# Two cost constants of a planner, and the order of TensorE's 965 units, in an attention and feed-forward kernel on one core

## The chip, the core and the metric

The kernel runs on one core of a Trainium2 chip. The metric is device time in microseconds (us) of one execution. The profile is that of one execution, with every instruction and every DMA packet of the core.

## What is computed

Eight batches of twelve heads, sequence 448, head dimension 64. Scores are mixed across heads before the softmax and again after it, and the result goes through a feed-forward layer with a squared ReLU:

```python
scores = scale * q @ k.T                              # (8, 12, 448, 448)
scores = einsum('bhij,hg->bgij', scores, w_pre)       # mix heads
attn   = softmax(scores)
attn   = einsum('bhij,hg->bgij', attn, w_post)        # mix heads again
x      = (attn @ v), heads side by side               # (3584, 768)
out    = relu(x @ w_in) ** 2 @ w_out                  # 768 -> 2048 -> 768
```

## The kernel before

**Work and its stages.** TensorE's work is cut into 965 units, each a few matmuls into one or two PSUM banks, plus warm-up matmuls that the planner puts into early gaps. The kinds of units, by the start of their names, with the lines that show them in the profile:

- `tr` (L832, L836): transposes of q and k of a batch.
- `spr` (L915): scores of the first 320 query rows of batch 0, made directly in the mixing layout.
- `qk` (L974, L981, L988): scores of a tile of 128 query rows, two heads at a time, six units a tile. A batch has four tiles; the fourth has 64 rows, is made by three units, and has line L974 to itself. Each score block is copied from PSUM into `stage` by ScalarE or VectorE (`fn_sev`).
- Relayout (`emit_rel`, `rel` tasks): DMAs issued by SyncE (SP) move ten query rows of all twelve heads from `stage` to a slot of `dring`, so that heads lie on partitions. Rows of a 128-row tile take one DMA (L1035); rows of the 64-row tile take two (L1033), here called split relayouts. A batch has eight of these.
- `pre` (L1059, L1066, L1074): the first head mixing, from `dring`. ScalarE makes the exponentials with their row sums (L1099), GpSimd (POOL) the reciprocal (L1122) and the scaled second mixing matrix (L1132).
- `post` (L1164): the second head mixing, which also transposes; its result goes to `a2t`.
- `av` (L1221, L1242): attention times v, to `xt`. `h` units (L1293, L1301): the first feed-forward matmul; its ReLU (L1338, L1339) and square (L1348) go to `h2t`. `o` units (L1440; L1380 and L1432 at the end): the second feed-forward matmul, a half of the contraction each. Its result goes to `osb` and is stored by SP (L1478).

Buffers that tie these together: `stage` has two slots, so a tile's copies wait until the relayouts of the tile before the last one have landed; `dring` has 16 slots; `osb` has two, so an output tile's copy waits until the store of the tile two before has landed.

**What sets the order.** No order is written by hand. At build time `_Plan` plays the program through with a cost for each task and gives every engine a list; semaphores are placed by those lists, and the chip runs each list in order. TensorE's sequence is a string, `ORDER`: each character names the stream (`s_T`, `s_QK`, `s_pre`, ...) from which the next unit is taken, and which of up to three array shapes it takes: whole array (`full`), halves by rows (`row`), or quarters (`quad`); `av` units have a shape of their own (`cols`), `spr` units too (`c32`). The string was found by a search that minimises the planned span. All other engines' lists follow from it in `run`: the next task is the one that can start first, and a copy goes to ScalarE or VectorE as the planner expects it to end sooner.

**The planner's costs that matter here.** A change of array shape between units costs `MODE_SWITCH`, 100 ns. TensorE's instructions come in blocks of 256; `fetch` says how long after entering a block the next one is there, with parts for loads and relayouts that are under way. Every relayout holds SP for 1000 ns, whether of one DMA or split:

```python
t = plan.add("rel%d_%d_%d" % (b, c, d0), SP, fn, sev_of[n],
             {SP: (1000.0, 0.0)}, g * 1.0, sem, 32 if two else 16,
             dma=("move", 10.0 + 73.3 * nv, 54.0))
```

The end of a relayout is the end of its modelled transfer plus `DMA_END["move"]` (`dma_next`).

Of the kernel before, what the change touches and what calls it, by code (L numbers as in the profile page):

```python
# [19 lines left out]
MODE_SWITCH = 100.0  # L20
ACT_BIAS = 14.5
BLOCK = 256
FETCH = (2700.0, 2300.0, 1500.0)
EVENTS = {"tr": 0.12, "qk": 0.72, "di": 0.2, "sp": 0.3, "po": 0.61, "pr": 1.1, "av": 0.43, "o0": 0.43}
DMA_START = {"move": 2590.0, "load": 2640.0, "big": 1680.0}
DMA_AHEAD = 1600.0
DMA_END = {"move": 1450.0, "load": 1300.0}
INF = float("inf")
CODES = "0123456789abcdefghijklmnopqrst"
ORDER = (  # L30
    "00005bb05b0555555555555555555c12c555555513223555552c5001c353c00153355255233355555b332c22"
    "44443002h1g1b2q1h332g2236gh313c6722133hh31233gh6131hb2424443b32g26gh7q2b7371c63q1711r736"
    "2qh32002932t121j33933282b2s3c83338004224441200bgh11181c3s311s133s322rghg22b72b6h3163q633"
    "q32r42244413rbbh2ggb2002h716371623763q223837c738c33i3832bgh112rg0204244b20041328111ic31i"
    "3c3i33911tc11t22bj3c393c39342414431j313j2bqb2b62731762236733h3200q2162r21h13633g32r22728"
    "02000s131i113i14242b4334222931t333t111922813i3138422443411i332q2b6b2r2brb2gq0023733r3633"
    "qbrbq2rg2r200bh22913j12009111j3c381c383c3s313sc342442224193139111t333t2422444228318131i3"
    "13s32q2bqr227b3h2b2g733q333q20b6r120h2q0262000h7119331t111j33ct2228383138131ib4242224418"
    "3138331i24244413832q2bq2r2bh236331q33hgb21g72000r102h2173633633h24244420ttb2092b9238111i"
    "133i333i2t22btb2btbb2t238338331i42244431s31q2262713r1161733qh32qb2g2r2b273733r33gg12s22i"  # L40
    "22ss42244483i33s33i2qr262h2933933t33jq4q444hgqg6rgqhrh7ihgh6hgrhgg7hrqjjsjjit8isitijj"
)


# [72 lines left out]
class _Plan:  # L117
# [86 lines left out]
    def dma_next(self, go=False):  # L204
# [26 lines left out]
        if go:  # L231
# [5 lines left out]
            self.moving[t.dma[0]].pop(0)  # L237
            t.end = max(t.end, now + DMA_END[t.dma[0]])
            self._finish(t)
# [10 lines left out]
    def fetch(self, at):  # L250
        part = {}
        for q, xs in self.moving.items():
            part[q] = min(1.0, sum(x[1] for x in xs if x[0] <= at + 500.0) / 2500.0)
        return FETCH[0] + FETCH[1] * part["load"] + FETCH[2] * part["move"]

# [1442 lines left out]
```

## Time and profile before

| | |
|---|---|
| Runs, median (lowest to highest of 3) | 539.58 us (534.83 to 539.79) |
| The profiled execution: its time, its span | 537.8 us, 536.0 us |
| Mean granted TensorE clock | 0.988 |
| Busy in the span: PE, ACT, DVE, POOL | 508.0, 412.3, 379.9, 290.8 us |
| Matmuls | 10441 |
| Instruction packets on the queue that serves TensorE | 86, of 16 KB |

The span runs from the first to the last instruction; the profiled execution's time is 1.8 us more. PE is TensorE's matmuls, SP the engine that only issues DMAs. "Idle before" names what ended a wait; "issue" means that the engine waited for nothing that the profile shows.

### The profile page before, as it was taken

To read this page: it belongs to the slowest core of one execution; us is meant where nothing else is said; L and a number is where in the kernel's file an instruction comes from. 1 tells how busy PE (TensorE), PEld (TensorE's weight loads), DVE (VectorE), ACT (ScalarE), POOL (GpSimd) and SP (SyncE) were. 2 spreads that over 40 slices of the span, in tenths; PEclk is the share of its full clock that TensorE was granted. 3 is DMA by queue.
4 is the path that set the end of the run, shared out by engine and by line. 5 is a ranking of instruction groups with operands and counts; after the bars stand their busy time and mean duration, and the time that the engine had idled before them with its cause. 6 is when DMAs were issued, how large, how long until landed. Compare 5 with 4: busy or idle time off the path is not lost.

```text
span 536.0 us, 24801 instructions
## 1 busy us (share of the span) xinstructions
PE 508.0 (95%) x10441; PEld 332.8 (62%) x10441; DVE 379.9 (71%) x806; ACT 412.3 (77%) x1181; POOL 290.8 (54%) x524
## 2 busy tenths in 40 slices
PE   8979999999999889989999899999989999989996
PEld 4435676667776546656566565666547766657963
DVE  7868977797987678765878768876857868536510
ACT  5979998888977878887787798888857888955421
POOL 9837788427954667446843587336844345522000
PEclk9989999999999999999999999999989999998999
DMA  9998999547964689457973689447963467532013
GB/s 172 192 184 145 196 183 193 112 87 146 178 154 75 137 183 173 93 127 135 180 166 67 140 150 224 92 91 163 193 134 64 105 141 142 113 72 61 3 29 93
DMA packets 81997, 70.87 MB, mean 132 GB/s; under 512 B 14038, under 2 KB 78422, under 8 KB 81878
## 3 DMA queue, kind: packets, MB, share of 16 engines
q1 hardware_dynamic: 48326, 46.40, 35.8%
q0 software_dynamic: 33392, 22.59, 31.0%
q8 instruction: 86, 1.41, 1.1%
q14 instruction: 33, 0.27, 0.1%
q10 hardware_dynamic: 160, 0.20, 0.1%
HBM read 45.63 MB, written 11.01 MB: 106 GB/s over the span
## 4 chain that ended last, share of the span: by engine, by line
PE 76%; DMA 7%; ACT 5%; DVE 4%; SPq 3%; issue 3%; POOL 0%; DVEq 0%; POOLq 0%
PE ps L1440 20%; PE ps L1301 17%; PE ps L1293 9%; PE ps L1164 6%; PE ps L1074 6%; DMA dring<-stage 5%; PE ps L1242 5%; SPq L1033 3%; ACT pring L1099 3%; PE ps L988 3%; PE ps L1380 2%; PE ps L1432 2%; PE ps L915 2%; DVE stage L524 2%; PE ps L836 2%
## 5 line engine op out<-in xcount | busy, mean ns | idle before, releaser
L1122 POOL TENSOR_TENSOR rinv<-rowsum,minus 128x2 f32<-128x2 f32 (+1 forms) x179 | 125.2, 702 | 185.9 <-ACT pring L1099 185.1
L1099 ACT ACTIVATE pring<-ps 128x448 bf16<-128x448 f32 x360 | 192.6, 563 | 23.0 <-PE ps L1074 13.2
L524 DVE CAST a2t<-ps 128x480 bf16<-128x480 f32 (+1 forms) x209 | 126.6, 641 | 37.6 <-PE ps L1164 36.7
L1440 PE MATMUL ps<-w_out_sb,h2t 64*128 64x384 bf16 (+1 forms) x1728 | 141.7, 324 | 0.2
L524 DVE CAST stage<-ps 128x448 bf16<-128x448 f32 x168 | 99.9, 618 | 31.1 <-PE ps L981 11.4
L1301 PE MATMUL ps<-xt,w_in_sb 64*64 64x448 bf16 (+4 forms) x1728 | 109.5, 329 | 0.1
L1440 PEld LDWEIGHTS ps<-w_out_sb,h2t 64*128 64x128 bf16 (+1 forms) x1728 | 75.3, 97 | 43.3 <-issue 2.0
L523 ACT ACTIVATE a2t<-ps 128x480 bf16<-128x480 f32 (+1 forms) x159 | 85.9, 580 | 20.8 <-PE ps L1164 20.0
L523 ACT ACTIVATE stage<-ps 128x448 bf16<-128x448 f32 x138 | 72.2, 556 | 18.7 <-PE ps L988 6.5
L1099 ACT ACTIVATION_READ_ACCUMULATOR pring<-ps 128x1 f32 x360 | 81.8, 227 | 0.0
L1301 PEld LDWEIGHTS ps<-xt,w_in_sb 64*64 64x64 bf16 (+1 forms) x1728 | 60.4, 103 | 29.8 <-issue 2.3
L1164 PEld LDWEIGHTS ps<-wk2s,pring 60*128 60x128 bf16 x2880 | 57.4, 94 | 28.0 <-issue 7.1
L1132 POOL TENSOR_TENSOR wk2s<-wk2b,rinv 128x120 bf16<-128x120 bf16 (+1 forms) x179 | 69.0, 388 | 10.2
L1164 PE MATMUL ps<-wk2s,pring 60*128 60x60 bf16 x2880 | 64.8, 187 | 4.4 <-issue 2.6
L1348 DVE TENSOR_TENSOR h2t<-h1t 128x448 bf16<-128x448 bf16 (+2 forms) x176 | 54.7, 336 | 11.2 <-ACT h1t L1338 10.1
L1074 PE MATMUL ps<-dring,wk 64*64 64x448 bf16 (+1 forms) x592 | 53.0, 360 | 10.0 <-DMA dring<-stage 3.4
L1293 PE MATMUL ps<-xt,w_in_sb 128*128 128x220 bf16 (+2 forms) x480 | 59.1, 276 | 0.0
L1338 ACT ACTIVATE h1t<-ps 128x448 bf16<-128x448 f32 (+2 forms) x88 | 39.1, 450 | 20.4 <-PE ps L1293 11.2
L1339 DVE TENSOR_SCALAR h1t<-ps 128x448 bf16<-128x448 f32 (+2 forms) x88 | 42.7, 492 | 16.5 <-PE ps L1301 13.1
L1293 PEld LDWEIGHTS ps<-xt,w_in_sb 128*128 128x128 bf16 x480 | 43.8, 98 | 12.3 <-issue 2.8
L523 ACT ACTIVATE osb<-ps 128x384 f32<-128x384 f32 x31 | 15.1, 492 | 27.2 <-PE ps L1432 8.6
L1242 PE MATMUL ps<-a2t,vraw 128*64 128x228 bf16 (+1 forms) x640 | 35.2, 261 | 0.0
(78 smaller groups left out, 464.5 us busy)
## 6 DMA issues: line engine op xcount, KB each, us to landing
dring<-stage SPq DMA_DIRECT2D x264, 105.0 KB
out_dram<-osb SPq DMA_DIRECT2D x45, 192.0 KB, 3.5
qraw<-in_q_dram POOLq DMA_DIRECT2D x42, 112.0 KB, 5.1
kraw<-in_k_dram POOLq DMA_DIRECT2D x42, 112.0 KB, 5.1
dring<-stage SPq DMA_DIRECT2D x70, 52.5 KB
w_in_sb<-in_moe_w_in_dram POOLq DMA_DIRECT2D x8, 384.0 KB, 10.0
w_out_sb<-in_moe_w_out_dram POOLq DMA_DIRECT2D x8, 384.0 KB, 8.8
vraw<-in_v_dram POOLq DMA_DIRECT2D x21, 128.0 KB
```

Of the source, the lines that this page charges most:

```text
L523: return eng.activation(o, i_, AF.Copy)
L524: return eng.tensor_copy(o, i_)
L1074: r_ = eng.matmul(ps[64 * y:64 * y + 64, gr.banks[x], 0:S], wk1[64 * x:64 * x + 64 - R0 * x, 64:128], dring[64 * x:64 * x + 64 - R0 * x, ( ...
L1099: return eng.activation(pring[:, pr, 0:S], ps[:, gr.banks[x], 0:S], AF.Exp, accum_out=rowsum[:, g, :])
L1122: return eng.tensor_tensor(rinv[:, p0:p0 + n, :], rowsum[:, g0:g0 + n, :], minus1[:, 0:n, :], ALU.pow)
L1132: return eng.tensor_tensor(wk2s[:, p0:p0 + n, :], i0.to_broadcast([128, n, PR]), rinv[:, p0:p0 + n, :].to_broadcast([128, n, PR]), ALU.mult)
L1164: r_ = eng.matmul(ps[:, gr.banks[x], o0:o0 + PR], pring[64 * x:64 * x + PR, pr + y, j0:j0 + 2 * PJ], wk2s[64 * x:64 * x + PR, pr + y, :], ...
L1242: r_ = eng.matmul(ps[kk * 64:kk * 64 + 64, g.banks[x_], x * n:(x + 1) * n], vraw[:, h, s, :], a2t[half][:, s, h, a0:a0 + n], start=(rest a ...
L1293: r_ = eng.matmul(ps[:, g.banks[ph], 0:n], w_in_sb[:, ft, t * 128:(t + 1) * 128], xt[:, ft, c0:c1], start=(ft == 0), stop=(ft == NFT - 1))
L1301: r_ = eng.matmul(ps[z:z + w, g.banks[x], 0:n], w_in_sb[64 * y:64 * y + 64, ft, t * 128 + z:t * 128 + z + w], xt[64 * y:64 * y + 64, ft, c ...
L1348: return eng.tensor_tensor(h2t[:, t16, o0:o0 + n], h1t[:, s, 0:n], h1t[:, s, 0:n], ALU.mult)
L1440: r_ = eng.matmul(ps[z:z + w, g.banks[hh], 0:FH], h2t[64 * y:64 * y + 64, t16, col + z:col + z + w], w_out_sb[64 * y:64 * y + 64, t16, hh ...
```

## The change

Two planner constants are raised: the base of an instruction fetch from 2700 to 3500 ns, and the time from a relayout's modelled end to its arrival from 1450 to 2000 ns. `ORDER` is replaced by another string of the same units. No other line differs, so all work is the same; what changes is its sequence on every engine, the array shapes of some units, and which of ScalarE and VectorE makes some copies.

```diff
-FETCH = (2700.0, 2300.0, 1500.0)
+FETCH = (3500.0, 2300.0, 1500.0)
...
-DMA_END = {"move": 1450.0, "load": 1300.0}
+DMA_END = {"move": 2000.0, "load": 1300.0}
...
 ORDER = (
-    "00005bb05b0555555555555555555c12c555555513223555552c5001c353c00153355255233355555b332c22"
+    "000b051010155555515555555555555c2552c5530055533c255553b22c50505553335c532c5535533155c4b4"
...
```

Two places show how the sequence moves.

The first is on PE where batch 2 ends and batch 3 begins. L974 with `qkt` is the 64-row score tile of batch 2; L988 and L981 are the score tiles of batch 3, six units each; L1440 is a half of an output tile, L1293 a piece of the first feed-forward matmul, L1074 the first head mixing. Before, from the last unit of the 64-row tile on:

```order
L974 MATMUL ps<-qkt 64x448 x8
L1074 MATMUL ps<-dring,wk 64x448 x4
L1293 MATMUL ps<-xt,w_in_sb 128x228 x12
L836 MATMUL ps<-ident,qraw 64x64 x28
L1074 MATMUL ps<-dring,wk 64x448 x4
L836 MATMUL ps<-ident,kraw 64x64 x28
L1221 MATMUL ps<-a2t,vraw 64x220 x8
L1074 MATMUL ps<-dring,wk 64x448 x4
L1242 MATMUL ps<-a2t,vraw 64x220 x24
L981 MATMUL ps<-qkt 64x448 x4
```

Now, from the same unit on:

```order
L974 MATMUL ps<-qkt 64x448 x4
L836 MATMUL ps<-ident,kraw 64x64 x28
L1221 MATMUL ps<-a2t,vraw 64x220 x8
L1074 MATMUL ps<-dring,wk 64x448 x4
L1242 MATMUL ps<-a2t,vraw 64x220 x24
L836 MATMUL ps<-ident,qraw 64x64 x28
L836 MATMUL ps<-ident,kraw 64x64 x28
L1074 MATMUL ps<-dring,wk 64x448 x4
L988 MATMUL ps<-qkt 128x448 x2
L1440 MATMUL ps<-w_out_sb,h2t 128x384 x16
L988 MATMUL ps<-qkt 128x448 x2
```

The feed-forward piece, a transpose and two head mixings now stand ahead of the 64-row tile; with them gone from behind it, the tiles of batch 3 follow it sooner.

The second is on SP at the same place. L1033 are the eight split relayouts of batch 2 (16 DMAs), L1035 the relayouts of whole tiles, L1478 the stores of output tiles (32 rows each for batch 0, 64 for batch 1). Before:

```order
L1035 DMA dring<-stage 48x1x448
L1478 DMA out_dram<-osb 32x768 x3
L1033 DMA dring<-stage 36x1x448 x2
L1033 DMA dring<-stage 60x1x448 x10
L1033 DMA dring<-stage 24x1x448 x4
L1478 DMA out_dram<-osb 32x768
L1478 DMA out_dram<-osb 64x768 x2
L1035 DMA dring<-stage 120x1x448 x12
```

Now:

```order
L1035 DMA dring<-stage 48x1x448
L1478 DMA out_dram<-osb 32x768 x4
L1478 DMA out_dram<-osb 64x768 x2
L1033 DMA dring<-stage 36x1x448 x2
L1033 DMA dring<-stage 60x1x448 x10
L1033 DMA dring<-stage 24x1x448 x4
L1035 DMA dring<-stage 120x1x448 x12
```

Three stores, among them the two of batch 1's first tile, moved from behind the split relayouts to ahead of them.

More of the change, by code (lines that the diff above doesn't have):

```diff
@@ L30 @@
 ORDER = (
-    "00005bb05b0555555555555555555c12c555555513223555552c5001c353c00153355255233355555b332c22"
[L32 to L41, printed above, removed]
+    "000b051010155555515555555555555c2552c5530055533c255553b22c50505553335c532c5535533155c4b4"
+    "4224300ch117311gq223h3c3rgc1631g2q3h2bc233rg311qh313hc242444332ghqh2gbb361736r1q172h61c6"
+    "73h32393b29b29b02093c38222i3s333s200244314240b20gq1118131i313i131822h7g31h22b2h6h33623q3"
+    "ch636314b44r242hbbg6b2002h7613g37c7373r36cqc8233821ci33i33gq221hh0104244002181218113i133"
+    "i3229319221t313t33422912jb4244b24339313t13qbb2g2711r3622763r33q2002g2r1b2712633q3300r227"
+    "282003i111s111s3342442b24223931j1139333j22831sb42442b438131i33q2b26r2bbh0022g633637336hb"
+    "qr12r2g2rb002h22933tc31j2001j11813381c1i1338242443342239221t3119333914242244238331sc8331"
+    "s32q2b6brb2372b2gh6333r100q2bq2r2337q2bq020002hh1192b39131j133jc338221s2318133i324142b24"
+    "4b22833824b444338133ib2qb2g2r2bh23633163hgb00227g02r0bbh263733q33h422444b29202093191j338"
+    "311s118311i1t22922tb2t23833i331842244423s31qbb2q2373613h2261713r33q22qr2b72q11q33733h2s2"
+    "42i2444i2i2283833i633i62q2293j33j33t46444h7hghhhi6hgrhqg6g8gg7h87h7hqgs8qhj9jjjiij8j9"
 )
```

## The prediction

> **What bounds the kernel now.** I read the page first, for the engine that carries the span, then that engine's waits, then the chain and the timeline at each longer wait.
>
> ```profile
> span 536.0 us, 24801 instructions
> PE 508.0 (95%) x10441; PEld 332.8 (62%) x10441; DVE 379.9 (71%) x806; ACT 412.3 (77%) x1181; POOL 290.8 (54%) x524
> ...
> PE 76%; DMA 7%; ACT 5%; DVE 4%; SPq 3%; issue 3%; POOL 0%; DVEq 0%; POOLq 0%
> ```
>
> PE is busy for 508 of 536 us and makes three quarters of the chain. The change keeps its work, so it can move two things: how often PE changes its array shape, and the 28 us in which PE stands. PE's own list of waits, with total, count and longest, has two kinds that the new constants concern, relayouts and waits for nothing visible:
>
> ```profile
> PE ps L1074 <- DMA dring<-stage: 3.4, 4, 1.6
> PE ps L974 <- issue: 2.8, 2, 2.6
> PE ps L1164 <- issue: 2.6, 2, 1.8
> PE ps L836 <- issue: 1.4, 1, 1.4
> ```
>
> The three rows of "issue" hold 6.8 us, nearly all in three stops that the chain shows in order of time:
>
> ```profile
> 26.52 1.39 issue
> ...
> 32.41 1.77 issue
> ...
> 393.59 2.65 issue
> ```
>
> Counting PE's instructions along the trace, each of these stops stands at the same place of a block of 256. They are waits for instructions. The first ends at 27.91, the second at 34.18: the next block took 6.27 us to come there, of which PE could work for only 4.5.
>
> A long stop is paid twice. Columns here are busy times by engine, then PEclk:
>
> ```profile
> 34.90:38.30 3.40, 3.40 (x35) 0.85 (x28) 1.49 (x4) 2.61 (x7) 0.00 (x0) 0.56 0.91 176
> ...
> 396.60:399.90 3.30, 3.30 (x37) 1.69 (x38) 1.88 (x4) 1.12 (x2) 0.00 (x0) 0.57 0.60 141
> ...
> 482.10:485.40 3.30, 3.27 (x44) 1.92 (x42) 1.06 (x3) 2.10 (x9) 2.98 (x6) 0.55 0.48 124
> ```
>
> The clock is granted at 0.55 to 0.57 for some 3.4 us just after the stops that end at 34.18, 396.24 and 481.18. With PE busy throughout, such a window loses about 3.4 x 0.44 = 1.5 us.
>
> **The change part by part.** *Shapes.* In PE's order, neighbouring units differ in shape 233 times before and 266 times in the change: 33 more. The price comes from one stretch of PE's timeline:
>
> ```profile
> 87.23 1.47 PE L1440 MATMUL ps<-w_out_sb,h2t 64*128 64x384 bf16 x16
> 88.54 0.39 PE L1164 MATMUL ps<-wk2s,pring 60*128 60x60 bf16 x16
> 88.86 0.38 PE L1074 MATMUL ps<-dring,wk 64*64 64x448 bf16 x4
> 89.17 1.48 PE L1440 MATMUL ps<-w_out_sb,h2t 64*128 64x384 bf16 x16
> 90.58 0.38 PE L974 MATMUL ps<-qkt 64*64 64x448 bf16 x4
> 90.79 0.36 PE L1074 MATMUL ps<-dring,wk 64*64 64x448 bf16 x4
> 90.98 0.36 PE L974 MATMUL ps<-qkt 64*64 64x448 bf16 x4
> ```
>
> From start to start, the output half takes 1.31 us when a unit of its own shape (64*128 and 60*128 are both halves by rows) follows, and 1.41 when a 64*64 one does. The head mixing takes 0.31 before another shape and 0.19 before its own. A change of shape costs 0.10 to 0.12 us: 33 x 0.115 = **+3.8**. The exchanged units, among them two more warm-up matmuls, add 0.2 by the same prices. Nothing hides this: PE is the chain. **+4.0**, bounds 3.5 to 4.5.
>
> *Instructions.* The change issues 172 fewer on PE (10355 matmuls, each with a weight load). With unit times as above and no stops, the blocks that end in the first two waits hold 4.6 and 4.0 us of work; the blocks in their place now hold 5.0 and 4.9, so these waits shrink by 0.4 and 0.9. In all, fewer blocks are short (under 5.0 us: 23 of 83 before, 16 of 82 now), for which I take 0.9, a third of the late wait of 2.65. **-2.2**. Bounds: all three long waits gone, -6.8; or one more of the longest kind with its halved clock, 2.65 + 1.5 = +4.2. I stay near the middle, as the rows show fetch time following DMA traffic, which the order does not remove.
>
> The Trainium skill, Runtime: NRT & Kernel Launch, "Instruction fetch mechanics", speaks against this term: it holds that the fetch of a next page is hidden by the sequencer's own pace per instruction. By that rule the term is nothing and the sum 2.2 higher. The three stops here disagree with it.
>
> *Output slots.* Twice an output tile's copy waits for its slot of `osb`, whose store stands in SP's queue behind split relayouts, and the copy, at the head of both copying engines, holds PE:
>
> ```profile
> 175.34 0.56 DVE L524 COPY osb<-ps 128x384 f32<-128x384 f32 x1 [0.61 <-DMA out_dram<-osb]
> ...
> 175.88 0.55 PE L988 MATMUL ps<-qkt 64*128 64x448 bf16 x4 [1.07 <-ACT osb L523]
> ...
> 467.27 9.28 SPq L1033 DMA_DIRECT2D dring<-stage  x12
> ...
> 480.56 0.56 DVE L524 COPY osb<-ps 128x384 f32<-128x384 f32 x1 [3.25 <-DMA out_dram<-osb]
> ...
> 481.18 0.38 PE L1074 MATMUL ps<-dring,wk 64*64 64x448 bf16 x4 [2.16 <-DVE osb L524]
> ```
>
> The SP order shows the stores of batch 1's first tile ahead of the split relayouts now, so the 1.07 goes. At the end of batch 6, two feed-forward pieces of 0.6 us move in ahead of the tile that waited, which takes 1.2 off the 2.16. **-2.3**; bounds 0, and all of it with the halved clock behind it, -4.7.
>
> *Batch boundaries.* This is what the new order does not account for. The planner lets every relayout hold SP for 1.0 us. The trace has:
>
> ```profile
> 116.39 6.36 SPq L1035 DMA_DIRECT2D dring<-stage  x7
> ...
> 155.75 0.57 PE L974 MATMUL ps<-qkt 64*64 64x448 bf16 x8
> ...
> 159.02 12.50 SPq L1033 DMA_DIRECT2D dring<-stage  x16
> 171.56 1.70 SPq L1478 DMA_DIRECT2D out_dram<-osb  x3
> ...
> 173.57 1.16 DVE L524 CAST stage<-ps 128x448 bf16<-128x448 f32 x2 [1.61 <-DMA dring<-stage]
> ...
> 174.26 0.55 PE L1066 MATMUL ps<-dring,wk 64*128 64x448 bf16 x4 [0.36 <-DVE stage L524]
> ```
>
> A whole relayout holds SP for 0.91 us, a split one for 12.50 / 8 = 1.56: eight of them take 4.5 us more than planned. From the last 64-row unit (ends 156.32) to the slot of `stage` being free (173.57) it takes 17.25 us. The next batch's second tile needs that slot. Batch 4 to 5 shows the same, 276.8 to 294.1:
>
> ```profile
> 276.43 0.38 PE L974 MATMUL ps<-qkt 64*64 64x448 bf16 x4
> ...
> 279.12 13.15 SPq L1033 DMA_DIRECT2D dring<-stage  x16
> ...
> 294.14 0.62 DVE L524 CAST stage<-ps 128x448 bf16<-128x448 f32 x1 [0.57 <-DMA dring<-stage]
> ...
> 294.83 0.40 PE L1164 MATMUL ps<-wk2s,pring 60*128 60x60 bf16 x16 [0.41 <-DVE stage L524]
> ...
> 299.05 0.38 PE L1074 MATMUL ps<-dring,wk 64*64 64x448 bf16 x4 [1.58 <-DMA dring<-stage]
> ```
>
> How much PE work stands in that gap? Adding units up to the end of the second tile's first one, I get for batches 1-2, 2-3, ... 6-7: before 15.6, 15.9, 20.7, 15.6, 19.4, 24.9 us; now 18.7, 12.7, 17.1, 14.1, 15.4, 21.3. The order's first place shows 2-3: a feed-forward piece, a transpose and head mixings have left the gap. Against 17.25, the two shown were late by 1.35 and 1.65 and cost PE 0.36 and 0.41, so PE loses the lateness less 1.1 (finished banks to work from). Now 2-3, 4-5 and 5-6 are late by 4.55, 3.15 and 1.85: 3.45 + 2.05 + 0.75 = 6.25, less the 0.77 of before, +5.5. What queues behind the waiting copy on both copying engines is the exponentials and the copies of the second mixing, and PE waits for those. In turn the next relayouts gain time: the 1.58 at 299.05 and 0.29 at 178.34, behind the same SP queue, can go, -1.9.
>
> ```profile
> 178.34 0.38 PE L1074 MATMUL ps<-dring,wk 64*64 64x448 bf16 x4 [0.29 <-DMA dring<-stage]
> ```
>
> **+3.6**. Bounds: the planned slack holds and the 0.77 goes too, -0.8; or nothing is given back and 2-3 waits for three more stores ahead of its splits (1.70 by the row above), +7.2, with two halved windows +10.2. I stay between, as the two late gaps in the trace cost less than their lateness.
>
> Sum: 4.0 - 2.2 - 2.3 + 3.6 = **+3.1** on the profiled execution's 537.8 (span 536.0, 1.8 around it). The runs' median of 539.6 lies 1.8 above that execution and takes the same addition: **542.7**.
>
> **The rivals.** *Split relayouts decide* (slower). If the gaps of 2-3 and 4-5 are paid in full, with three more stores ahead, nothing given back and a halved window after each stop over 2 us, the sum is 3.1 + 1.9 + 1.7 + 3.0 = +9.7: 549.3. It decides once lateness passes some 2 us. For it: the 4.5 us that the planner misses a batch, and gaps of 12.7 and 14.1. Against it: 1-2 is relaxed by 3 us, and whole relayouts are planned 0.09 us too dear, 38 a batch.
>
> *The reserve works* (faster). All three long instruction waits go with the two halved windows behind them (-9.8), the slots bring 2.3, and the boundaries cost nothing: 4.0 - 9.8 - 2.3 = -8.1: 531.5. For it: the waits are real and short blocks fewer. Against it: the +4.0 is certain, and the boundary gaps shrink.
>
> *The fetch reserve brings nothing*: short blocks move, and as many waits stay, as the rows cannot tell which blocks meet heavy traffic. Then +5.3: 544.9. This is the time that the page's rule gives too, though for another reason.
>
> **How the numbers follow.** Forecast 0.40, split relayouts 0.38, reserve 0.16, no fetch gain 0.06. A measurement of this kernel can tell about 1% from no change, 5.4 us: same is 534.2 to 545.0. The last case lies at that edge and is halved: faster 0.16, same 0.43, slower 0.41. The forecast's own range is 537 to 547. The range over the cases is 532 to 553: it leaves out the lower half of the fast case and the outer end of the slow one, where both bounds of boundaries and fetches meet.
>
> **What would show it.** Right: changes of shape keep their 0.10 to 0.12; the second tile's copies of batches 3 and 5 wait 2 us or more on `dring<-stage`, with PE idle behind `stage`; no wait on `osb` near batch 3's start; waits on "issue" near 4 to 5 us in sum. Wrong: no stop at the boundaries, which ends the +3.6 and with it the slow side; or PE's "issue" total at 2 us or under, or above 9.

## The result: no difference

| | before | changed |
|---|---|---|
| Median of 20 runs each (lowest to highest) | 538.27 us (532.34 to 539.79) | 536.68 us (534.62 to 542.04) |
| Ratio, 95% interval | | 1.0002 [0.9975, 1.0029] |
| Profiled execution: time, span | 537.8, 536.0 us | 534.62, 532.1 us |

The forecast was 542.7, with 537 to 547 for its own case and 532 to 553 over all cases. The time lies just under the first and inside the second, but the 3.1 us that were forecast are not there: the interval ends at +0.29%, 1.6 us. Of the 6.0 us between 542.7 and 536.68, 1.3 are the base, because the forecast adds to a median of 539.6 over three runs. The two medians differ by 1.6 us, the means of the same runs by 0.1 (537.5 and 537.6). Both kernels spread over some 7 us from run to run, and the profiled execution of the changed kernel is at the low end of its runs, so single pairs of traces are read here for where time goes, and ratios for how much.

The page of the changed kernel, its span, busy times and the engines' shares of the chain:

```profile
span 532.1 us, 24620 instructions
PE 510.1 (96%) x10355; PEld 329.8 (62%) x10355; DVE 377.8 (71%) x802; ACT 415.9 (78%) x1185; POOL 290.7 (55%) x524
...
PE 75%; SPq 7%; DMA 6%; DVE 5%; ACT 4%; issue 2%; DVEq 0%; ACTq 0%
```

PE is busy for 2.1 us more on 86 fewer matmuls, although it has one halved window less (below), so the changes of shape show. SP's own queue now has 7% of the chain, where it had 3%.

PE's waits of the changed kernel (total, count, longest; all rows that name `stage`, `dring`, `osb` or "issue"):

```profile
PE ps L1074 <- DMA dring<-stage: 4.4, 3, 2.0
PE ps L1164 <- DVE stage L524: 3.9, 3, 3.0
PE ps L1164 <- issue: 3.1, 4, 1.7
...
PE ps L1074 <- DVE stage L524: 0.8, 1, 0.8
PE ps L1242 <- issue: 0.7, 1, 0.7
PE ps L1301 <- issue: 0.6, 1, 0.6
PE ps L1293 <- issue: 0.4, 1, 0.4
PE ps L988 <- ACT stage L523: 0.4, 2, 0.2
...
PE ps L1066 <- DMA dring<-stage: 0.3, 1, 0.3
PE ps L836 <- issue: 0.3, 1, 0.3
...
PE ps L988 <- DVE stage L524: 0.2, 1, 0.2
```

And of the kernel before, those rows that the prediction did not show:

```profile
PE ps L1074 <- DVE osb L524: 3.1, 2, 2.2
...
PE ps L1164 <- DVE stage L524: 1.4, 2, 1.0
...
PE ps L988 <- ACT osb L523: 1.1, 1, 1.1
PE ps L1074 <- DVE stage L524: 0.9, 2, 0.7
...
PE ps L1066 <- DVE stage L524: 0.4, 1, 0.4
PE ps L1074 <- issue: 0.4, 1, 0.4
PE ps L915 <- issue: 0.3, 1, 0.3
PE ps L981 <- issue: 0.3, 1, 0.3
```

The long ones among the waits on `stage`, `dring` and `osb` end with a DMA that SP issues, which PE itself or the copy ahead of it waits for. Added up, with the prediction's rows, these are 10.3 us before and 10.0 now: `osb` has gone (4.2 to 0), `stage` and `dring` have taken its place. The rows of "issue", instruction waits, sum to 7.8 before and 5.1 now. Such sums are good to about 1 us: one row of before, 1.00 us put to `stage` at 67.49, stands at the place of a block of 256 where the instruction waits stand, and may be one.

The two boundaries that the prediction named as tight do stop PE, on the timeline of the changed kernel:

```profile
161.89 12.62 SPq L1033 DMA_DIRECT2D dring<-stage  x16
...
176.40 0.62 DVE L524 CAST stage<-ps 128x448 bf16<-128x448 f32 x1 [3.05 <-DMA dring<-stage]
...
176.42 0.38 PE L1074 MATMUL ps<-dring,wk 64*64 64x448 bf16 x2 [1.97 <-DMA dring<-stage]
...
279.86 12.69 SPq L1033 DMA_DIRECT2D dring<-stage  x16
...
294.51 1.69 DVE L524 CAST stage<-ps 128x448 bf16<-128x448 f32 x3 [3.41 <-DMA dring<-stage]
...
295.73 0.40 PE L1164 MATMUL ps<-wk2s,pring 60*128 60x60 bf16 x16 [3.00 <-DVE stage L524]
```

Each is followed by the halved clock (busy times by engine, then PEclk), two windows where the kernel before had three:

```profile
176.80:180.20 3.40, 3.21 (x30) 1.61 (x32) 1.38 (x3) 1.72 (x7) 2.13 (x5) 0.53 0.54 112
295.60:299.00 3.40, 3.27 (x48) 1.69 (x48) 2.29 (x5) 1.24 (x3) 0.00 (x0) 0.62 0.53 103
```

One part of the profiled execution's lead is none of the change's doing. From PE's last matmul to the end of the span, with only copies and stores left, it takes 5.1 us before and 3.5 now. In the other traces it is 3.7 to 5.7, with either order, so 1.6 us of the lead is the draw of one execution.

### The profile page after: what moved, and what is told of

The parts are those of the page before. It is cut to its first block, busy times and chain, and to the rows that moved or that the text cites. A ratio compares the mean times of both kernels' runs of the same rounds, so it can differ in the third digit from the quotient of the medians.

```text
span 532.1 us, 24620 instructions
## 1 busy us (share of the span) xinstructions
PE 510.1 (96%) x10355; PEld 329.8 (62%) x10355; DVE 377.8 (71%) x802; ACT 415.9 (78%) x1185; POOL 290.7 (55%) x524
## 4 chain that ended last, share of the span: by engine, by line
PE 75%; SPq 7%; DMA 6%; DVE 5%; ACT 4%; issue 2%; DVEq 0%; ACTq 0%
PE ps L1440 18%; PE ps L1301 16%; PE ps L1293 8%; PE ps L1164 6%; DMA dring<-stage 6%; PE ps L1242 6%; PE ps L1074 5%; SPq L1033 5%; PE ps L988 3%; PE ps L1380 2%; PE ps L1432 2%; DVE stage L524 2%; PE ps L915 2%; PE ps L836 2%; SPq L1035 1%
## 5 line engine op out<-in xcount | busy, mean ns | idle before, releaser
L524 DVE CAST a2t<-ps 128x480 bf16<-128x480 f32 (+1 forms) x205 | 123.7, 639 | 31.8 <-PE ps L1164 31.5
L1440 PE MATMUL ps<-w_out_sb,h2t 64*128 64x384 bf16 (+1 forms) x1664 | 143.2, 326 | 0.1
L524 DVE CAST stage<-ps 128x448 bf16<-128x448 f32 x172 | 101.8, 618 | 38.8 <-PE ps L981 10.7
L1301 PE MATMUL ps<-xt,w_in_sb 64*64 64x448 bf16 (+4 forms) x1704 | 109.3, 329 | 0.7 <-issue 0.6
L1440 PEld LDWEIGHTS ps<-w_out_sb,h2t 64*128 64x128 bf16 (+1 forms) x1664 | 74.0, 96 | 46.4 <-issue 3.1
L523 ACT ACTIVATE a2t<-ps 128x480 bf16<-128x480 f32 (+1 forms) x163 | 88.0, 579 | 17.6 <-PE ps L1164 17.1
L523 ACT ACTIVATE stage<-ps 128x448 bf16<-128x448 f32 x134 | 69.3, 548 | 23.4 <-PE ps L988 10.5
L1099 ACT ACTIVATION_READ_ACCUMULATOR pring<-ps 128x1 f32 x360 | 79.5, 221 | 0.0
L1301 PEld LDWEIGHTS ps<-xt,w_in_sb 64*64 64x64 bf16 (+1 forms) x1704 | 59.9, 102 | 29.9 <-issue 2.4
L1164 PEld LDWEIGHTS ps<-wk2s,pring 60*128 60x128 bf16 x2880 | 55.5, 94 | 30.3 <-issue 6.9
L1164 PE MATMUL ps<-wk2s,pring 60*128 60x60 bf16 x2880 | 63.2, 187 | 7.1 <-DVE stage L524 3.9
L1348 DVE TENSOR_TENSOR h2t<-h1t 128x448 bf16<-128x448 bf16 (+2 forms) x176 | 56.4, 343 | 18.2 <-ACT h1t L1338 17.3
L1293 PE MATMUL ps<-xt,w_in_sb 128*128 128x220 bf16 (+2 forms) x480 | 58.8, 274 | 0.5 <-issue 0.4
L1074 PE MATMUL ps<-dring,wk 64*64 64x448 bf16 (+1 forms) x598 | 53.8, 362 | 5.3 <-DMA dring<-stage 4.4
L1339 DVE TENSOR_SCALAR h1t<-ps 128x448 bf16<-128x448 f32 (+2 forms) x91 | 43.6, 491 | 14.0 <-PE ps L1301 10.3
L1293 PEld LDWEIGHTS ps<-xt,w_in_sb 128*128 128x128 bf16 x480 | 43.7, 98 | 12.7 <-issue 2.3
L737 POOL DMA_DIRECT2D vraw<-in_v_dram x54 | 33.9, 634 | 2.9 <-PE ps L1242 2.5
```

The lines of the kernel that those rows point to most:

```text
L523: return eng.activation(o, i_, AF.Copy)
L524: return eng.tensor_copy(o, i_)
L1074: r_ = eng.matmul(ps[64 * y:64 * y + 64, gr.banks[x], 0:S], wk1[64 * x:64 * x + 64 - R0 * x, 64:128], dring[64 * x:64 * x + 64 - R0 * x, ( ...
L1099: return eng.activation(pring[:, pr, 0:S], ps[:, gr.banks[x], 0:S], AF.Exp, accum_out=rowsum[:, g, :])
L1164: r_ = eng.matmul(ps[:, gr.banks[x], o0:o0 + PR], pring[64 * x:64 * x + PR, pr + y, j0:j0 + 2 * PJ], wk2s[64 * x:64 * x + PR, pr + y, :], ...
L1293: r_ = eng.matmul(ps[:, g.banks[ph], 0:n], w_in_sb[:, ft, t * 128:(t + 1) * 128], xt[:, ft, c0:c1], start=(ft == 0), stop=(ft == NFT - 1))
```

## The experiments

Ratios are against runs of the kernel before on the same chip, made together with those of the experiment.

**Which half of the change does anything?** `const_only` has the old order with the new constants, `order_only` the new order with the old constants (the diff is the two constants, or the string, alone).

> Before's order string with the two raised constants. TensorE's sequence of units and shapes is before's; only the copies' engines and SP's places can move. If the result comes from the order of the units (theory), this is before's time within 2 us (538), with shape changes as before. If the constants act by themselves through the other engines' lists (rival), a part of the fewer stops of the change appears here: 533 to 535.

> The changed order string with the old constants. Theory: as the change, 537, with 266 shape changes and the same clean sum of units (4.0 us above before's). Rival (the constants matter): the stops of the change come back and the time is before's plus 2 to 4: 540 to 542.

Measured: 1.0017 [0.9976, 1.0059], 537.71 us, and 0.9971 [0.9927, 1.0016], 536.94. Neither differs from the kernel before by more than 0.7%, the outer ends of the intervals. Neither the constants nor the order by itself moves the time by anything that can be told from nothing. Since the waits differ all the same, losses and gains of the order would have to cancel, and the next runs take them apart.

The constants do move SP's list: with the old ones, two stores stand behind the split relayouts of batch 2 again, and PE waits for `osb` near batch 3's start (L1074) and at the end of batch 6 (L1301), where the changed kernel has no such row. From `order_only`:

```profile
173.56 1.69 SPq L1478 DMA_DIRECT2D out_dram<-osb  x2
```

```profile
PE ps L1301 <- ACT osb L523: 2.1, 1, 2.1
PE ps L1074 <- ACT osb L523: 2.1, 1, 2.1
```

Its rows on `osb`, `stage` and `dring` sum to 10.1 us all the same, where the changed kernel has 10.0.

**What do the split relayouts cost each order?** `half_split_after` and `half_split_before` issue one DMA of the two:

```diff
-                    for y in range(2 if two else 0):
+                    for y in range(1 if two else 0):
...
-                             {SP: (1000.0, 0.0)}, g * 1.0, sem, 32 if two else 16,
+                             {SP: (1000.0, 0.0)}, g * 1.0, sem, 16,
```

> The changed kernel with only one of the two DMAs of each split relayout: six of the twelve heads of a batch's last 64 rows are left out. If the split relayouts on SP set the stops at the batch boundaries (theory), these stops, 9.4 us in the profile and 2 us of halved clock, go nearly all: 526 to 530. If the boundaries wait for the copies or for loads (rival), under 3 us: 534 or more.

> Before with only one of the two DMAs of each split relayout, the same part left out. Theory: the stops at the boundaries (7.7 us) and the two waits for an output slot behind the splits (3.2 and 1.5 of halved clock) go: 527 to 531. Rival: under 3 us, 535 or more. If the two orders differ by their boundaries, this one gains less than the changed kernel does.

Measured: 0.9673 [0.9580, 0.9765], 519.58 us, and 0.9662 [0.9590, 0.9734], 520.15 us. Both gain some 18 us, about twice what was expected. The intervals are 5 and 4 us wide to each side, so the times could not show a difference of +3.6 between the orders. The rows of PE's waits that name "issue" and the longest of the others, first with the order before, then with the new one:

```profile
PE ps L1164 <- issue: 2.7, 3, 1.8
PE ps L974 <- issue: 2.4, 1, 2.4
...
PE ps L836 <- issue: 1.4, 1, 1.4
PE ps L915 <- issue: 1.2, 1, 1.2
PE ps L981 <- issue: 0.8, 1, 0.8
PE ps L1164 <- DVE h2t L1348: 0.6, 1, 0.6
```

```profile
PE ps L1164 <- issue: 3.7, 4, 1.7
...
PE ps L1301 <- issue: 0.6, 1, 0.6
...
PE ps L915 <- issue: 0.2, 1, 0.2
PE ps L988 <- ACT stage L523: 0.2, 1, 0.2
```

No row names `osb` or `dring` any more, and one names `stage`, with 0.2 us. So the rows that go sum to 10.3 us with the order before and 9.8 with the new one: by them the new order did not lose more to SP's queue, where the prediction had -2.3 and +3.6.

**SP's time, or the bytes?** In that pair half the bytes went too. In the next two kernels all bytes stay, and POOL issues the second DMA. The planner's cost of each half is 800 ns, so its lists can shift a little too:

```diff
+                    en = POOL if y else SP
...
-                t = plan.add("rel%d_%d_%d" % (b, c, d0), SP, fn, sev_of[n],
-                             {SP: (1000.0, 0.0)}, g * 1.0, sem, 32 if two else 16,
+                    t = plan.add("rel%d_%d_%d_%d" % (b, c, d0, y), en, fn, sev_of[n],
+                                 {en: (800.0 if two else 1000.0, 0.0)}, g * 1.0, sy, 16,
```

> The changed kernel with the second of the two DMAs of each split relayout issued by POOL, which is idle for about half of a boundary, and no longer by SP. All the work stays, all bytes too. Theory A (SP's time to issue binds the boundaries): SP is relieved of 8 x 0.78 = 6.2 us at each of six boundaries, as when that DMA was left out (519.6), so nearly all of the 17 us comes: 520 to 526, no stop of 2 us or more behind dring<-stage or stage, and PE stands some 16 us over its unit times instead of 31. Rival B (moving the bytes binds, issue does not): the DMA engines carry as much as before, 533 to 539. Rival C (POOL's row sums and scales of the softmax wait behind the DMAs it must now issue): what SP gains comes back as PE waits behind pring or wk2s, above 537.

> The kernel before with the same edit (second DMA of each split relayout from POOL). Theory A: 520 to 527, close to split_pool_after, because in the changed kernel 4.0 us more of shape changes stand against 4 to 9 us less of instruction waits and halved clock. Were the changed order's fetch reserve worth what the half-split pair's traces showed (15.4 us of fetch and halved clock against 6.5), it would be 3 to 5 us above split_pool_after. Rival B: 534 to 540, as for the other.

Measured: 0.9933 [0.9904, 0.9962], 533.31 us, and 0.9788 [0.9750, 0.9825], 526.28 us. With the order before, theory A holds: 11 us (9 to 13 by the interval) come from moving half of these DMAs off SP, the bytes unchanged, and no wait on `osb`, `stage` or `dring` is left in PE's list. With the new order the time misses theory A's 520 to 526. What is missing to `half_split_before`, 6.4 us between the spans of the two traces, stands mostly behind POOL: 4.1 us of PE's waits name `wk2s`, and there are two halved windows more, 3.0 us. POOL's queue and PE, order before:

```profile
99.28 4.56 POOL L1039 DMA_DIRECT2D dring<-stage  x8
103.86 0.40 POOL L1140 TENSOR_TENSOR wk2s<-wk2b,rinv 128x120 bf16<-128x120 bf16 x1
```

```profile
104.32 0.58 PE L1172 MATMUL ps<-wk2s,pring 60*128 60x60 bf16 x16 [3.04 <-POOL wk2s L1140]
105.98 0.58 PE L1172 MATMUL ps<-wk2s,pring 60*128 60x60 bf16 x16 [1.08 <-POOL wk2s L1140]
```

With the new order a load of k is late, in the same way:

```profile
273.28 1.82 POOL L1039 DMA_DIRECT2D dring<-stage  x3
275.51 2.77 POOL L1039 DMA_DIRECT2D dring<-stage  x5 [0.41 <-issue]
...
283.30 0.67 POOL L699 DMA_DIRECT2D kraw<-in_k_dram  x1
```

```profile
286.26 0.59 PE L837 MATMUL ps<-ident,kraw 64*64 64x64 bf16 x28 [5.09 <-DMA kraw<-in_k_dram]
```

The next kernels leave the batch that suffers to SP (`en = POOL if y and b != 4 else SP`; `b != 1`; `b not in (1, 4)`).

> The changed kernel with the second DMAs of split relayouts on POOL as in split_pool_after, but those of batch 4 left on SP, so that batch 5's last load of k is not queued behind them on POOL. Theory (split_pool_after lost its gain to that one load, 5.1 us of wait and two thirds of a window of halved clock, beside 4.5 us behind POOL's wk2s): without it 528 to 530, and a stop behind stage or dring<-stage near 295 comes back, 2 to 3 us of it already counted. Rival (the changed order's own tight boundaries keep it slow whoever issues): 532 to 534.

> split_pool_before (526.3) with batch 1's second DMAs left on SP. In its trace POOL issued all eight in one piece of 4.6 us and PE then lost 6.5 us near 105 (3.4 and 1.4 behind wk2s and most of a window of halved clock); on SP that boundary cost 2 us. Theory: 521 to 524. Rival (that loss falls in a place where another wait takes over): 525 to 528.

> split_pool_after_not4 (527.2) with batch 1's second DMAs on SP too. POOL's loss near 102 was 3.8 us with the halved clock in it, SP's there 2.3. Theory: 525 to 527, so the two orders differ by 2 to 5 us in favour of the order before once neither SP nor POOL holds them up, as unit times and block ends together say they should be equal (504.1 each) and the new order keeps batch 4's splits on SP. Rival (the new order is better at the boundaries): 521 to 524.

Measured: 0.9834 [0.9790, 0.9879], 527.18 us; 0.9839 [0.9789, 0.9889], 525.10 us; 0.9904 [0.9865, 0.9943], 530.13 us. The late load explains the new order's lag: with batch 4 on SP it gains 5 us and cannot be told from `split_pool_before` any more. Batch 1 does not follow the theory: giving it back to SP gains nothing that shows in the order before, and the new order loses 4 us by the ratios; why, no run shows. The lowest ratio of a kernel that does all the work is that of `split_pool_before`, 2.1% under the kernel before, and it keeps the order before.

**What is a change of shape worth?** Two kernels keep an order of units and choose other shapes (only the string's codes for shapes differ), then the same on the order before with SP relieved.

> The changed kernel's order of units with other array shapes chosen for the same units: 209 changes of shape instead of 266, at 764 more instructions on PE (22086 instead of 21322, three more blocks of 256). Theory (a change of shape costs 0.115 us, on PE's own chain): -57 x 0.115 + 5 head mixings by rows x 0.19 = -5.6, so 531. Rival (three more blocks and other places of the block ends bring instruction waits of 1.5 to 2.7 us each, halved clock behind): 535 to 540.

> The kernel before, same order of units, with shapes chosen so that it changes shape 302 times instead of 233, at 396 fewer instructions on PE (21098 instead of 21494). Theory (0.115 us each, paid in full): +69 x 0.115 = +7.9, so 546. Rival (fewer, fuller blocks give it back in instruction waits): 538 to 541.

> many_before (302 changes of shape instead of 233, same order of units) with the second DMAs of split relayouts on POOL; it stands against split_pool_before, 526.3. Unit times and changes of shape sum to 501.1 us instead of 493.1. Theory A (a change of shape costs its 0.115 us whenever PE is the bound; in many_before half was hidden in stops behind SP): with SP relieved the whole +8.0 shows, 533 to 535. Rival B (other engines pace PE everywhere, so half of what PE's own work gains or loses is taken back in waits): +4, 529 to 531.

> The kernel before's order of units with 190 changes of shape instead of 233 and 700 more instructions on PE, the second DMAs of split relayouts on POOL; it stands against split_pool_before, 526.3. Unit times and changes of shape sum to 488.1 us instead of 493.1. Theory A (shape changes are paid in full): -5.0, 521. Rival B (700 instructions more make more blocks short: 15 under 4.5 us after 85 us instead of 8, short of 5 us by 20.6 in sum instead of 9.7, and in the first 85 us short of 6 us by 14.1 instead of 8.7): instruction waits grow by 5 to 12 us, so 526 to 533.

Measured, with what the expectations took from unit times and changes of shape alone:

| kernel | changes of shape | by unit times | against | measured |
|---|---|---|---|---|
| many_before | 302, were 233 | +8.0 us | before | 1.0059 [1.0022, 1.0097]: +3.2 us |
| many_split_before | 302, were 233 | +8.0 us | split_pool_before | 0.9973 [0.9938, 1.0008] to 0.9788: +9.9 us |
| few_after | 209, were 266 | -5.6 us | changed kernel | 1.0063 [1.0027, 1.0099] to 1.0002: +3.3 us |
| few_split_before | 190, were 233 | -5.0 us | split_pool_before | 0.9985 [0.9949, 1.0021] to 0.9788: +10.6 us |

While SP's queue stops PE, adding changes cost 3.2 us of 8.0 (1.2 to 5.2 by the interval). With SP relieved the rise is 9.9, but that cannot be put down to the changes of shape: the kernel with fewer changes rises by as much, 10.6. A line of the page of many_before, and its longest stop with what led to it:

```profile
PE 514.7 (95%) x10243; PEld 329.4 (61%) x10243; DVE 381.8 (70%) x806; ACT 412.3 (76%) x1181; POOL 290.8 (54%) x524
```

```profile
175.69 1.20 SPq L1478 DMA_DIRECT2D out_dram<-osb  x2
...
178.96 0.49 ACT L523 ACTIVATE osb<-ps 128x384 f32<-128x384 f32 x1 [4.44 <-DMA out_dram<-osb]
...
179.51 0.56 PE L988 MATMUL ps<-qkt 64*128 64x448 bf16 x2 [4.22 <-ACT osb L523]
```

PE is busy for 6.7 us more, with three halved windows as before, so the price is real: 0.10 us a change. Its longest stop is for a store on SP, and its rows on `osb`, `stage` and `dring` sum to 8.1 us, 2.2 less than before, which may be where a part of the price is taken back. Taking changes away did not pay at all: fewer changes of these shapes need 700 to 764 more instructions, and the time rises. In `few_after` the unit prices themselves miss: PE is busy for 511.5 us, 1.4 more than in the changed kernel and not 5.6 less, with two halved windows in each, while its listed waits sum to 18.0 us as the changed kernel's do. Where the rest of its 3.3 us goes is not settled.

**Where the blocks end.** If the reserve for fetches is what places the block ends well, then moving all of them by 128 instructions should undo it. Short warm-up matmuls ahead of the first transpose do that:

```diff
+                    for _ in range(tiny):
+                        r_ = eng.matmul(ps[0:64, g.banks[0], 0:64], warm[0:64, 0:64],
+                                        warm[0:64, 0:64], start=True, stop=True)
-                    for _ in range(n):
+                    for _ in range(n - 4 if tiny else n):
```

(`tiny` is 68; 136 for 8 long ones in the second; in the last two 75 for all 11.)

> The changed kernel with 68 short warm-up matmuls in place of 4 long ones ahead of the first transpose, where PE waits for the first load anyway: every later unit keeps its place, shape and order, and the ends of all blocks of 256 instructions move 128 instructions forward. Theory (what the changed order gained at instruction waits lies in where its block ends fall): at the traced unit times the blocks in the program's first 85 us fall short of 6 us by 8.3 us in sum instead of 5.0, and after that 10 blocks instead of 6 are under 4.5 us, falling short of 5 us by 14.8 instead of 6.9. So instruction waits and the halved clock behind them grow by 4 to 8 us: 541 to 545. Rival (which blocks are late follows the traffic of the moment, and what one loses another hides): 535 to 539, as the changed kernel.

> The changed kernel with 136 short warm-up matmuls in place of 8 long ones: 256 instructions more ahead of the first transpose, so from then on every block ends at the same instruction as in the changed kernel. Theory (shift_after was slow by where its blocks ended, not by its warm-up): 536 to 539, with at most one stop of 2 us in the first 10 us, where one block more has to come, and after that the stops of the changed kernel. Rival (short warm-up matmuls themselves cost time, through the clock or the start): 542 or more.

> The kernel before with the warm-up of shift_after: block ends 128 instructions forward. At the traced unit times the blocks fall short of 6 us (first 85 us) by 11.0 instead of 8.7 and of 5 us (after that) by 19.1 instead of 9.7. Theory (0.6 us of time for each us of shortfall, as shift_after's +5.5 for 11.1): +7.0, so 543 to 546. Rival (the order before was already poorly placed, its stops cannot get worse): 536 to 540.

Measured: 1.0117 [1.0079, 1.0156], 542.19 us; 1.0121 [1.0050, 1.0193], 541.67 us; 1.0014 [0.9970, 1.0057], 536.52 us. The first agreed with the theory, but the control with all ends back in place came out as slow. So the theory cannot take the 6 us for itself. One thing that the edit brings is a late start. The start of PE in shift_after, shift256_after and the changed kernel:

```profile
1.44 3.83 PE L662 MATMUL ps<-warm 64*64 64x64 bf16 x68 [1.44 <-DVE warm L645]
...
7.93 0.96 PE L837 MATMUL ps<-ident,qraw 64*64 64x64 bf16 x28
```

```profile
1.44 7.46 PE L662 MATMUL ps<-warm 64*64 64x64 bf16 x136 [1.44 <-DVE warm L645]
...
10.06 0.95 PE L837 MATMUL ps<-ident,qraw 64*64 64x64 bf16 x28
```

```profile
5.66 0.88 PE L832 MATMUL ps<-ident,qraw 64*64 64x64 bf16 x28
```

A short matmul takes 56 ns there (3.83 / 68), and the first transpose comes 2.3 and 4.4 us late. That is not the whole of the 6 us: in shift_before the first transpose comes 2.8 us late (7.93 after 5.14), and the time rises by 0.8 us, 3.1 at the interval's end. Two more runs take the late start away.

> As shift_after, with 75 short warm-up matmuls in place of all 11 long ones: at 55 ns each they take 4.1 us where the long ones took 3.8 to 4.3, so the first transpose starts as before, and all block ends stand 128 instructions forward. Theory (0.6 us for each us of shortfall of the blocks, 22.9 instead of 12.0): +6.6, 541 to 544. Rival (what shift_after lost beyond its late start, 5.5 - 2.3): +3, 539 to 540. Second rival (where blocks end is worth nothing on the whole): 535 to 538.

> The same in the order before: shortfall 30.1 instead of 18.4. Theory: +7, 542 to 545. Rival (shift_before less its late start of 3.1): -2 to -3, 533 to 536, which would say that the shortfall at unit prices does not tell which block ends are good.

Measured: 1.0028 [0.9984, 1.0071], 538.73 us, and 0.9995 [0.9958, 1.0031], 535.52 us. Moving every block end by 128 changes neither order by anything that can be told from nothing; the theory of shortfalls, +6.6 and +7, falls. The sums of the "issue" rows stay too: 4.2 us in shift_early_after, 8.0 in shift_early_before. What made shift_after and shift256_after slow beyond the late start stays open.

## Why the prediction was wrong, step by step

PE's waits of the executions, summed from their lists as above ("SP" are the rows on `osb`, `stage` and `dring<-stage`), and the windows of halved clock of some 3.4 us with PE at work:

| order | execution | SP | of it `osb` | "issue" | windows |
|---|---|---|---|---|---|
| before | before | 10.3 | 4.2 | 7.8 | 3 |
| before | const_only | 12.2 | 2.8 | 5.9 | 1 |
| before | shift_before, shift_early_before | 10.9, 9.6 | 5.0, 4.7 | 6.2, 8.0 | 0, 1 |
| before | half_split_before, split_pool_before, split_pool_before_not1 | 0, 0, 2.5 | 0, 0, 0 | 8.5, 7.7, 6.2 | 2, 4, 2 |
| new | changed | 10.0 | 0 | 5.1 | 2 |
| new | order_only | 10.1 | 4.2 | 4.9 | 3 |
| new | shift_after, shift256_after, shift_early_after | 10.3, 12.1, 10.2 | 1.2, 2.0, 1.5 | 4.0, 2.0, 4.2 | 4, 2, 4 |
| new | half_split_after, split_pool_after, _not4, _not14 | 0.2, 0.2, 0.8, 2.0 | 0, 0, 0.6, 1.4 | 4.5, 6.9, 3.0, 6.4 | 0, 2, 2, 0 |

The first four executions of the order before and the first five of the new one, which leave both DMAs of a split relayout to SP, tell what each order loses to SP's queue; all rows tell about instructions and the clock. The kernels with other shapes, many_ and few_, are not in the table.

- **Batch boundaries, +3.6: the failed step.** By the rows on `stage` and `dring` they cost 2.2 us (6.6 on the mean with the order before, 8.8 with the new one). The new side of the sum was right: the loss behind `stage` was put at 6.25, and its rows have 6.4 on the mean. The named stops came too: the copies of batches 3 and 5 waited 3.05 and 3.41 us, and PE lost 1.97 and 3.00, where 3.45 and 2.05 were forecast, the first of them at a head mixing whose own relayout landed together with the slot of `stage` (176.42 and 176.40); the third, 0.75, has no row. What was wrong is the other side, "less the 0.77 of before": the list of the kernel before names `stage` with 2.7 us, of which the prediction counted two stops (1.00 of the rest is the doubtful row at 67.49), and the mean of the order before is 3.4. So the loss rises by 3.0 and not by 5.5. What was to come back on `dring`, -1.9, is -0.8 on the mean.
- **Output slots, -2.3: right on the mean, and not a term of its own.** The rows on `osb` fall from 4.2 to 1.8, by 2.4. But the same order has 0 in the changed kernel and 4.2 in `order_only`, while all of SP's rows sum to 10.0 and 10.1. SP is late by what the split relayouts hold it, since the rows go to 0 and 0.2 when half of these DMAs leave SP, and an order, with the constants, chooses which copy meets that lateness. Slots and boundaries together were to cost +1.3; measured is -0.2 (10.8 to 10.5 on the mean). `half_split` agrees within its intervals: both orders gain some 18 us when one DMA of each pair goes.
- **Instructions, -2.2: right in size.** The "issue" rows average 7.2 us over seven executions of the order before and 4.6 over nine of the new one: -2.6. The long wait of 2.65 is gone in the changed kernel; the longest is 1.7. The sum of 5.1 is where the text put it, 4 to 5. The reason given, short blocks, is not shown: the sums keep their difference when all block ends move. Nor do the constants bring it when the order is played through: `order_only`, with the old ones, has 4.9. Whether the search found this string because of the higher reserve, no run shows. One bound was misread: the three long stops are 5.8 us in sum and the rows 6.8, so "all three gone" is worth 1.0 less. The rule of the Trainium skill, Runtime: NRT & Kernel Launch, "Instruction fetch mechanics", that fetches are hidden, disagrees with every execution of the table: 2.0 to 8.5 us of PE's waits.
- **Shapes, +4.0: held, with a limit.** Six pairs differ in the order and have the same edit (changed and before, order_only and const_only, half_split, split_pool, shift, shift_early). PE's busy time rises by 2.1, 6.3, 1.9, 1.3, 8.9 and 7.3 us; with 1.5 us set off for each halved window by which a pair differs, by 3.6, 3.3, 4.9, 4.3, 2.9 and 2.8, on the mean 3.6. "Nothing hides this" is too strong: with SP in the way, 69 more changes made PE busy for 6.7 us more and cost 3.2. How much of this change's 3.6 is taken back in that way was not measured by itself.
- **The halved clock: left out, and no difference.** The likeliest sum held nothing for it. The windows number 13 in the seven executions of the order before and 19 in the nine of the new one: 1.86 and 2.11 on the mean, +0.4 us at 1.5 each. The mean granted clock says the same: 0.989 over the 20 runs of the changed kernel, 0.990 over 116 runs of the kernel before beside the experiments.

With these sizes the sum is 3.6 - 2.6 - 2.4 + 2.2 + 0.4 = +1.2 us instead of +3.1; the ratio's interval is -1.3 to +1.6 us. Of the 1.9 between, 1.4 are the boundaries. The sum goes by traces of single executions, which differ by several us, so that gains and losses cancel is what they add up to and not what one experiment isolates.

The signs that the prediction named as right were there in the changed kernel: a change of shape at 3.6 / 33 = 0.11, the two copies' waits, no wait on `osb` near batch 3's start, "issue" at 5.1. The time still did not rise, because none of the signs weighed what the same queue cost the order before.

Of the rivals, "split relayouts decide" named the queue that holds the kernel but not that it holds both orders alike. "The reserve works" had the direction of the instruction waits, at 2.6 of its 9.8 us, and the windows did not go. "The fetch reserve brings nothing" is against the rows, although they do not show that it is the reserve that brings it.

## What to carry to other kernels

Before pricing an order, ask which queue ends the waits of both orders, and price that queue's own time once: here one DMA more per split relayout on SP cost 11 us in the order before (9 in the new one, with batch 4 left on SP), and giving it to another queue did what no order did. Take what a wait costs before from the list of all waits and not from the stops that come to mind, since the difference hangs on both sides. An experiment that shifts things needs a control that shifts back: without it, the first shifted run would have passed as proof of the theory.

## What the hardware showed that was not expected

- POOL issued a half of a split relayout in 0.57 us (4.56 / 8), SP in 0.79 (12.62 / 16).
- A 64x64 matmul of the warm-up took 56 ns at the start of the program, and a transpose of that shape 22 ns (0.63 / 28) a few us later. What sets the two apart, no run here shows.
- In the changed kernel and the one before, PE's instruction stops of 0.25 us and more all stand at the same place of a block of 256, and PE goes on 1.3 to 1.6 us after the packet of the instruction queue has ended; the new order has 85 such packets, the one before 86, so it is not their number that tells the two apart.
